# Four token groups taken by pairs, with seven block products for eight, in a fused attention and channel-MLP kernel

## The chip, the cores and the metric

One core of a Trainium2 chip runs the whole program. The metric is the device time of one execution in microseconds. Three executions of the kernel before took 926.74, 927.08 and 929.66 us; the median, 927.08 us, is the time to compare with. About 0.3% (2.8 us) is what a measurement of this kernel can tell from no change.

## The reference

Inputs are eight batches of 576 tokens. Attention has 8 heads of 64 and is cut into chunks of 64 tokens; its output `x` (576 tokens by 512 channels) goes through a low-rank token mixer and a two-layer channel network:

```python
scores = scale * (q_c @ k_c^T)               # per chunk of 64 tokens
attn = softmax(scores); out = attn @ v_c
x = out.transpose(0, 2, 1, 3).reshape(B, S, 512)
h = xt @ U @ V                               # rank 32, over the tokens; xt is x transposed
u = x + h
out = u + relu(u @ w_ch1) @ w_ch2            # 512 -> 2048 -> 512
```

U, V and the two weight matrices come as float64 words, which the kernel rounds to float32 itself.

## The kernel before, in words

**Tiles and groups.** Batches go in four pairs. A pair has 1152 tokens: 9 tiles of 128, or 3 groups of 384. The 2048 hidden channels are 16 blocks of 128, numbered f. For a group and a block, `hidden` (L850) makes 128 hidden channels by 384 tokens in one PSUM bank, `relu_high` (L858, ScalarE) and `relu_low` (L863, VectorE) evacuate it, and `project_out` (L876) adds the block's share to three open output banks. There are 12 groups, so 192 such blocks.

**Three products for one.** TensorE takes float32r. To keep float32's precision each operand is split into a high part (a rounded copy, a CAST on ScalarE) and a low part (the difference, on VectorE), and a product is three matmuls: high by high, high by low, low by high. So `hidden` is 4 slices of 128 input channels x 3 = 12 matmuls of 384 columns, and `project_out` is 3 tiles x 3 = 9 matmuls of 512 columns. All split weights stay in SBUF (`w1[f]`, `w2[f]`), with no more transfers after the first stage.

**Order of the work.** The first 32 blocks are ordered by a planner (`order`), together with the loads, the weights' rounding and the first pair's attention. After it the program is written block by block. A tick is a quarter of a block (`now` counts them, 4 to a block, 64 to a group) and `agenda` holds what else is recorded at a tick: the attention of the later pairs (`Tile`), the mixer (`Mix`, `project_ops`), and their transfers. `at(s, ...)` books a step. In each engine's queue instructions run in the order in which they were recorded.

**Attention of a later pair.** `permute` reorders q and k through DRAM, `load` reads them (L699), `turn` transposes in 32x32 blocks on VectorE (L707), `visit` makes the scores of two tiles and the values of the two before (L724, L777), `softmax`, `turn_ex`, `put_ex` and `get_ex` bring the exponentials through DRAM into the transposed form. `load_v` (L714) is issued by POOL. The fourth pair's visits stand at ticks 410, 454, 518, 538 and 582; the fourth pair's own groups run from tick 576.

**The last four groups** are group 2 of the third pair and groups 0 to 2 of the fourth: 64 of the 192 blocks, from tick 512 on. They run as all others do.

## Time and profile before

| What | Value |
|---|---|
| median of three runs | 927.08 us |
| span of the profiled execution | 927.1 us |
| TensorE busy | 908.8 us, 98% |
| VectorE busy | 455.5 us, 49% |
| ScalarE busy | 226.0 us, 24% |
| GpSimd busy | 84.7 us, 9% |
| DMA | 100.09 MB, mean 108 GB/s |

The profiled execution's span and the median differ by less than 0.1 us, so a sum made against the span can be read against the median. PE stands for TensorE, PEld for its weight loads, DVE for VectorE, ACT for ScalarE, POOL for GpSimd, and L with a number is a line of the kernel. A busy PE is not PE at its peak: matmuls overlap, so the time of one is read from the distance between two starts, not from its length.

### The profile page before, as it was taken

To read this page: it belongs to the slowest core of one execution; us is meant where nothing else is said; L and a number is where in the kernel's file an instruction comes from. 1 tells how busy PE (TensorE), PEld (TensorE's weight loads), DVE (VectorE), ACT (ScalarE), POOL (GpSimd) and SP (SyncE) were. 2 spreads that over 40 slices of the span, in tenths; PEclk is the share of its full clock that TensorE was granted. 3 is DMA by queue.
4 is the path that set the end of the run, shared out by engine and by line. 5 is a ranking of instruction groups with operands and counts; after the bars stand their busy time and mean duration, and the time that the engine had idled before them with its cause. 6 is when DMAs were issued, how large, how long until landed. Compare 5 with 4: busy or idle time off the path is not lost.

```text
span 927.1 us, 16326 instructions
## 1 busy us (share of the span) xinstructions
PE 908.8 (98%) x6596; PEld 806.3 (87%) x6596; DVE 455.5 (49%) x901; ACT 226.0 (24%) x399; POOL 84.7 (9%) x157
## 2 busy tenths in 40 slices
PE   6899999999999999999999999999999999999998
PEld 5568888888888888998898888998889889898987
DVE  4799995575455445426554455433554342321111
ACT  5576751121221221111221211111121121111110
POOL 4300000222021020202021001020103000000000
PEclk9999999999999999999999999999999999999999
DMA  9894695776387373433567546152517102110000
GB/s 181 189 322 136 155 226 103 151 197 125 53 186 164 52 175 79 108 62 102 76 148 165 89 99 169 40 131 58 103 23 168 38 3 67 57 46 1 35 1 35
DMA packets 281115, 100.09 MB, mean 108 GB/s; under 512 B 206448, under 2 KB 268432, under 8 KB 281040
## 3 DMA queue, kind: packets, MB, share of 16 engines
q1 hardware_dynamic: 165440, 76.19, 33.2%
q10 hardware_dynamic: 111360, 14.16, 9.7%
q0 software_dynamic: 4240, 8.71, 3.7%
q8 instruction: 52, 0.85, 0.4%
q14 instruction: 23, 0.19, 0.1%
HBM read 74.63 MB, written 38.54 MB: 122 GB/s over the span
## 4 chain that ended last, share of the span: by engine, by line
PE 88%; DMA 4%; DVE 3%; ACT 2%; issue 2%; SPq 1%; POOL 1%; ACTq 0%; POOLq 0%
PE o L876 41%; PE h L850 41%; DMA qkv<-in_q_dram 3%; PE as L724 2%; PE as L777 1%; DMA qkv<-in_v_dram 1%; PE u L637 1%; DVE wroom L106 1%; PE y L591 1%; PE y L590 1%; SPq L423 1%; DVE wraw L103 1%; ACT w L375 1%; DVE x L888 0%; ACT wraw L96 0%
## 5 line engine op out<-in xcount | busy, mean ns | idle before, releaser
L850 PE MATMUL h<-uth,w 128*128 128x384 f32 x1536 | 423.7, 338 | 0.0
L876 PE MATMUL o<-w,hh 128*128 128x512 f32 x1152 | 362.9, 396 | 0.6 <-ACT hh L858 0.5
L850 PEld LDWEIGHTS h<-uth,w 128*128 128x128 f32 x1536 | 281.1, 188 | 8.0 <-issue 0.2
L863 DVE SCALAR_TENSOR_TENSOR hl<-h,hh 128x384 fp32r<-128x384 f32 x192 | 106.3, 554 | 366.2 <-ACT hh L858 366.2
L850 PE MATMUL h<-utl,w 128*128 128x384 f32 x768 | 259.6, 338 | 0.0
L876 PEld LDWEIGHTS o<-w,hh 128*128 128x128 f32 x1152 | 213.3, 188 | 37.6 <-ACT hh L858 1.6
L876 PE MATMUL o<-w,hl 128*128 128x512 f32 x576 | 227.7, 395 | 0.6 <-DVE hl L863 0.5
L858 ACT ACTIVATE hh<-h 128x384 fp32r<-128x384 f32 x192 | 93.8, 489 | 547.8 <-PE h L850 542.3
L850 PEld LDWEIGHTS h<-utl,w 128*128 128x128 f32 x768 | 144.2, 188 | 8.3 <-issue 0.2
L876 PEld LDWEIGHTS o<-w,hl 128*128 128x128 f32 x576 | 108.2, 188 | 28.0 <-DVE hl L863 2.5
L714 POOL DMA_DIRECT2D vn<-in_v_dram x108 | 65.9, 619 | 603.1 <-DVE sm L750 131.7
L744 ACT ACTIVATE ex<-ex 128x512 f32<-128x512 f32 x27 | 17.1, 632 | 82.5 <-DVE ex L738 77.2
L737 DVE TENSOR_REDUCE mx<-as 128x4 f32<-128x256 f32 x54 | 22.5, 416 | 27.2 <-PE as L777 25.6
L888 DVE TENSOR_TENSOR x<-o,x 128x512 f32<-128x512 f32 x48 | 30.3, 679 | 1.7 <-PE o L876 1.7
L707 DVE STREAM_TRANSPOSE qT<-qn 128x512 f32<-128x512 f32 x27 | 19.0, 705 | 22.3 <-DMA qn<-qblocks 17.4
L643 DVE TENSOR_TENSOR x<-u,x 128x512 f32<-128x512 f32 x36 | 23.9, 669 | 6.6 <-PE u L637 6.6
L840 DVE TENSOR_TENSOR utl<-uf,uth 128x512 fp32r<-128x512 f32 x30 | 19.8, 675 | 11.4 <-ACT uth L839 11.3
L738 DVE TENSOR_TENSOR ex<-as,mx 128x256 f32<-128x256 f32 x54 | 22.9, 424 | 1.9
L839 ACT CAST uth<-uf 128x512 fp32r<-128x512 f32 x30 | 18.3, 618 | 21.2 <-DMA uf<-xs 21.1
L812 DVE STREAM_TRANSPOSE xb<-x 128x512 f32<-128x512 f32 x30 | 21.2, 708 | 0.7
L93 ACT ACTIVATE wroom<-wraw 128x1024 f32<-128x1024 f32 (+1 forms) x19 | 19.0, 998 | 8.9 <-issue 4.8
L707 DVE STREAM_TRANSPOSE kT<-kn 128x512 f32<-128x512 f32 x27 | 18.6, 690 | 4.6 <-DMA kn<-kblocks 4.2
(89 smaller groups left out, 505.8 us busy)
## 6 DMA issues: line engine op xcount, KB each, us to landing
wraw<-in_moe_w_ch_dram SPq DMA_DIRECT2D x32, 512.0 KB, 6.0
out_dram<-x SPq DMA_DIRECT2D x36, 256.0 KB, 2.3
xs<-xb SPq DMA_DIRECT2D x120, 64.0 KB, 1.8
uf<-xs SPq DMA_DIRECT2D x30, 256.0 KB, 3.3
qblocks<-in_q_dram ACTq DMA_DIRECT2D x24, 288.0 KB, 4.0
kblocks<-in_k_dram ACTq DMA_DIRECT2D x24, 288.0 KB, 5.1
vn<-in_v_dram POOLq DMA_DIRECT2D x108, 64.0 KB, 3.6
exs<-exb SPq DMA_DIRECT2D x108, 64.0 KB, 2.2
```

Source lines behind the costliest of these rows:

```text
L643: nc.vector.tensor_add(x, st["u"], x)
L707: nc.vector.transpose(dst.rearrange("p a b -> p (a b)"), src.rearrange("p a i d -> p (a i d)"))
L714: nc.gpsimd.dma_start(self.vn[e * C : (e + 1) * C, c], v[b + 2 * self.pr, HP * e : HP * (e + 1), s0 : s0 + C, :].rearrange("h s d -> s h d"),)
L737: nc.vector.reduce_max(mx[:, e], self.sc[e].rearrange("p (h k) -> p h k", k=C), axis=AX.X)
L738: nc.vector.tensor_sub(self.ex[:, e].rearrange("p b h k -> p h b k"), self.sc[e].rearrange("p (h b k) -> p h b k", b=2, k=TB), mx[:, e].un ...
L812: nc.vector.transpose(self.xb.rearrange("p g (c t) -> p c g t", t=TB), x_of[self.pr, self.t].rearrange("p (c g k) -> p c g k", g=NQ, k=TB),)
L840: nc.vector.tensor_sub(ul, self.uf, uh)
L850: nc.tensor.matmul(ps[:, :GN], lhsT=w[:, z, cc], rhs=u[:, cc, :], start=(n == 0), stop=(n == 3 * NCC - 1))
L858: nc.scalar.activation(hh, ps[:, :GN], AF.Relu)
L863: nc.vector.scalar_tensor_tensor(hl, ps[:, :GN], 0.0, hh, op0=ALU.max, op1=ALU.subtract)
L876: nc.tensor.matmul(acc[j], lhsT=h[:, js], rhs=w2[f][:, z], start=(first and i == 0), stop=(final and i == 2),)
L888: nc.vector.tensor_add(x, ps, x)
```

## The change

**Block products.** The last four groups are taken as two pairs of groups (`JOINT`, s = 0 and 1). For two blocks of hidden channels (2i and 2i+1), two halves of 256 input channels and two groups, plain work needs 8 products of 256 channels x 128 x 384. The new code forms sums and differences of the weight quarters and of the token quarters and needs 7 (k = 1 to 7), each 6 matmuls of 384 columns. The results are joined in PSUM: ScalarE copies a partial sum out of a bank (`snap`, L1453), VectorE adds it onto another bank (`add`, L1456), and the next product goes on accumulating in the bank that was copied.

**Weights' sums.** `combos` forms them on POOL (three of the 16 first adds on VectorE) in the 64 ticks before tick 512 and writes them to DRAM as float32. In the joint part each of 2 x 4 x 14 products streams one 128x256 piece back (`issue`, 11 buffers deep) and splits it (`split_w`): a CAST on ScalarE (L1366), and a subtraction (L1367), 107 of 112 times on POOL. `Combos` does the same for the tokens' sums (POOL) and their 21 splits per pair (ScalarE L1418, VectorE L1419).

**A chunk.** A joint part is 4 chunks of 4 hidden blocks. `STEPS` gives the order on PE: A and B are the two pairs of hidden blocks, the digit is the product, Ga and Gb are the output matmuls (6 each, 12 steps).

**Attention.** The fourth pair's visits move to ticks 366, 394, 420, 446 and 480, the third pair's from 218 to 390 become 221.5 to 346. Tiles of `x` of both pairs are written to DRAM (`spill`) and read again (`fetch`, `store`, `residual`), since there are only 9 buffers. `turn` and `turn_ex` transpose in place. A table (`TUNE`) shifts single steps and names the issuing queue of single transfers.

The core of the diff:

```diff
...
+        "cget 0.1.0": -16, "cget 0.1.1": -6, "cget 1.0.0": -16, "cget 1.0.1": -17,
+        "clo 0.1.2": "S", "clo 0.1.5": "S", "clo 1.0.3": "S", "clo 1.0.6": "S", "clo 1.2.3": "P",
...
+    JOINED = 8 * NF * 4
+    LOADS = 11
+    AHEAD = 5
...
+    STEPS = "A1 A5 A2 A6 A3 B1 A7 B5 A4 B2 B6 B3 Ga0 B7 Ga1 B4 Gb0 Gb1 Ga2 Gb2 Ga3 Gb3 Ga4 Gb4 Ga5 Gb5".split()
+    CHUNKS = NF // 4
+    JOINT = [((2, 2), (3, 0)), ((3, 1), (3, 2))]
...
+            a, z = slice(0, KC), slice(KC, DM)
+            nc.gpsimd.tensor_sub(r1[:, a], two[:, a], one[:, a])
+            nc.gpsimd.tensor_sub(r2[:, z], two[:, z], two[:, a])
+            nc.gpsimd.tensor_sub(r2[:, a], two[:, z], r1[:, a])
+            nc.gpsimd.tensor_sub(r1[:, z], one[:, z], r2[:, a])
+
+        def put():
+            done.add(("put", i))
+            if not i % 2:
+                wc[i // 2] = dram.tile([P, len(ORDER), KC], F32, name=f"wc_{i // 2}")
+            to = wc[i // 2]
+            one, two, r1, r2 = st["b"]
+            for src, ks in ((one, (1, 2)), (two[:, KC:], (3,)), (r1, (5, 4)), (r2, (6, 7))):
+                at = [ORDER.index("AB"[i % 2] + str(k)) for k in ks]
+                dma(
+                    "wput",
+                    to[:, at[0] : at[-1] + 1 : max(1, at[-1] - at[0])],
+                    src.rearrange("p (k x) -> p k x", x=KC),
+                    i,
+                )
+
...
+    def split_w(n):
+        if n >= BLOCKS_OF * len(JOINT):
+            return
+        assert ("issue", n) in done
+        done.add(("wsplit", n))
+        h, l = window(n)
+        nc.scalar.copy(h, l.bitcast(F32))
+        side("wlo", n).tensor_sub(l, l.bitcast(F32), h)
+
...
+            if k == 5:
+                self.sums[j] = slot(F32, f"us_{self.s}_{j}", (P, 2, NQ, 2, TB))
+            one, two = (self.sums[j][:, z] for z in range(2))
+            dst = {5: one, 6: two, 3: one, 7: two}[k]
+            if k == 5:
+                nc.gpsimd.tensor_add(dst, b[:, :, 0:2], half[4])
+            elif k == 6:
+                nc.gpsimd.tensor_sub(dst, one, half[1])
+            elif k == 3:
+                nc.gpsimd.tensor_sub(dst, half[2], two)
...
+            def snap(z, b, name):
+                t = st[z, name] = temp(f"{name}_{s}_{c}{z}")
+                nc.scalar.copy(t, bank_of(z, b))
+
+            def add(z, b, name):
+                nc.vector.tensor_add(bank_of(z, b), bank_of(z, b), st[z, name])
+
...
+                for step, run in (
+                    (p1, lambda z=z: snap(z, "x", "s1")),
+                    (p5, lambda z=z: snap(z, "c", "s5")),
+                    (p2, lambda z=z: add(z, "y", "s1")),
+                    (p6, lambda z=z: snap(z, "x", "u2")),
+                    (p6, lambda z=z: relu(z, 0, bank_of(z, "y"))),
+                    (p3, lambda z=z: add(z, "c", "u2")),
+                    (x1, lambda z=z: relu(z, 1, bank_of(z, "c"))),
+                    (p7, lambda z=z: snap(z, "x", "u3")),
+                    (p7, lambda z=z: last_join(z)),
+                    (x2, lambda z=z: relu(z, 3, st[z, "u3"])),
+                    (p4, lambda z=z: relu(z, 2, bank_of(z, "x"))),
+                ):
...
+                    z, k = step[0], int(step[1])
+                    n = loads[0]
+                    loads[0] += 1
+                    w = [v.rearrange("p (c f) -> p c f", c=2) for v in window(n)]
...
+                    for cc in range(2):
+                        for m, (wz, uz) in enumerate(((0, 0), (0, 1), (1, 0))):
+                            nc.tensor.matmul(
+                                ps,
+                                lhsT=w[wz][:, cc],
+                                rhs=u[uz][:, cc],
+                                start=(k in (1, 2, 5) and cc == 0 and m == 0),
+                                stop=(cc == 1 and m == 2),
+                                skip_group_check=True,
+                            )
...
+                    if n + LOADS < BLOCKS_OF * len(JOINT):
+                        at(f"issue {n + LOADS}", now, lambda n=n: issue(n + LOADS))
...
+    VISITS = [
+        (94, 1, 0), (114, 1, 2), (138, 1, 4), (158, 1, 6), (198, 1, 8),
+        (221.5, 2, 0), (262, 2, 2), (290, 2, 4), (318, 2, 6), (346, 2, 8),
+        (366, 3, 0), (394, 3, 2), (420, 3, 4), (446, 3, 6), (480, 3, 8),
+    ]
...
+    for pr, g in ((0, 2), (1, 0), (1, 1), (1, 2), (2, 0), (2, 1)):
+        for f in range(NF):
+            ps = hidden(pr, g, f)
+            hh = relu_high(pr, g, f, ps)
+            hs = hh, relu_low(pr, g, f, ps, hh)
+            for j in range(GT + 1):
+                tick()
+                if j < GT:
+                    flush(j)
+            pend = (pr, g, f, hs)
+    for n in range(7, LOADS):
+        issue(n)
+    for s, groups in enumerate(JOINT):
+        joint(s, groups)
...
```

**What moves on PE.** PE in the last groups, before: the end of a block's hidden matmuls and its output matmuls (`h` is the hidden bank, `uth` and `utl` the tokens' high and low parts, `o` an output bank, `hh` and `hl` the hidden parts; in square brackets what an instruction waits for).

```order
L850 MATMUL h_2_15_8938<-uth_2_8257,w_1649 128x384 x2
L850 MATMUL h_2_15_8938<-utl_2_8258,w_1649 128x384
L850 MATMUL h_2_15_8938<-uth_2_8257,w_1649 128x384
L876 MATMUL o_6_8588<-w_1607,hh_2_14_8925 128x512 [waits Activation_49]
L876 MATMUL o_6_8588<-w_1607,hh_2_14_8925 128x512
L876 MATMUL o_6_8588<-w_1607,hl_2_14_8927 128x512 [waits DVE_49]
L876 MATMUL o_7_8592<-w_1607,hh_2_14_8925 128x512 x2
L876 MATMUL o_7_8592<-w_1607,hl_2_14_8927 128x512
L876 MATMUL o_8_8596<-w_1607,hh_2_14_8925 128x512 x2
L876 MATMUL o_8_8596<-w_1607,hl_2_14_8927 128x512
```

PE in the second chunk of the first joint part: products 5 of B and 4 of A (`c_1B` and `x_1A` are PSUM banks, every `w` is a piece of the freed weight area that holds a split weight piece or a split token sum).

```order
L1524 MATMUL c_1B<-w_1021,w_1649 128x384 [waits DVE_49,Activation_49]
L1524 MATMUL c_1B<-w_1082,w_1649 128x384
L1524 MATMUL c_1B<-w_1021,w_1649 128x384 [waits Pool_49]
L1524 MATMUL c_1B<-w_1021,w_1649 128x384
L1524 MATMUL c_1B<-w_1082,w_1649 128x384
L1524 MATMUL c_1B<-w_1021,w_1649 128x384
L1524 MATMUL x_1A<-w_1500,w_614 128x384 [waits Activation_49]
L1524 MATMUL x_1A<-w_1550,w_614 128x384
L1524 MATMUL x_1A<-w_1500,w_951 128x384 [waits Pool_49]
L1524 MATMUL x_1A<-w_1500,w_614 128x384
L1524 MATMUL x_1A<-w_1550,w_614 128x384
L1524 MATMUL x_1A<-w_1500,w_951 128x384
```

The 12 matmuls of one bank became two products of 6 in two banks; product 4 goes on in the bank `x_1A`, and its first matmul waits for ScalarE.

**What moves on ScalarE.** ACT in the last group, before: one evacuation a block and nothing else.

```order
L858 ACTIVATE hh_2_3_8639<-h_2_3_8626 128x384 [waits DVE_49,PE_49]
L858 ACTIVATE hh_2_4_8665<-h_2_4_8652 128x384 [waits DVE_49,PE_49]
L858 ACTIVATE hh_2_5_8691<-h_2_5_8678 128x384 [waits DVE_49,PE_49]
L858 ACTIVATE hh_2_6_8717<-h_2_6_8704 128x384 [waits DVE_49,PE_49]
L858 ACTIVATE hh_2_7_8743<-h_2_7_8730 128x384 [waits DVE_49,PE_49]
```

ACT in the second chunk of the first joint part (COPY is `snap`, the CAST from `w` to `w` is the weights' split, ACTIVATE the relu).

```order
L1453 COPY s_0_1A<-x_1A 128x384 [waits PE_49]
L1366 CAST w_1607<-w_1607 128x256 [waits DMAHW1_49]
L1453 COPY s_0_1A<-c_1A 128x384 [waits PE_49,Activation_49]
L1453 COPY u_0_1A<-x_1A 128x384 [waits PE_49]
L1465 ACTIVATE hh_1A<-y_1A 128x384 [waits DVE_49]
L1366 CAST w_1649<-w_1649 128x256 [waits DMAHW3_49]
L1366 CAST w_614<-w_951 128x256 [waits DMAHW6_49,Pool_49]
L1366 CAST w_1021<-w_1082 128x256 [waits DMAHW7_49,Pool_49]
L1465 ACTIVATE hh_1A<-c_1A 128x384 [waits DVE_49]
L1453 COPY s_0_1B<-x_1B 128x384 [waits PE_49,Activation_49]
L1453 COPY u_0_1A<-x_1A 128x384 [waits PE_49,Activation_49]
L1366 CAST w_1128<-w_1160 128x256 [waits DMAHW4_49,Pool_49]
```

Copies of banks, weights' splits that wait for a transfer, and relus now stand in one queue.

**What moves on POOL.** POOL before: the last steps it has are issues of v loads.

```order
L714 DMA vn_7_7407<-in_v_dram 64x4x64 [waits DMASW3_49,DVE_49,Activation_49]
L714 DMA vn_7_7407<-in_v_dram 64x4x64 [waits DMASW4_49]
L714 DMA vn_7_7407<-in_v_dram 64x4x64 [waits DMASW5_49]
L714 DMA vn_7_7407<-in_v_dram 64x4x64 [waits DMASW6_49]
L714 DMA vn_8_7642<-in_v_dram 64x4x64 [waits DMAHW2_49,DMAHW1_49,DMAHW3_49,DMASW7_49,DMAHW4_49,DVE_49,PE_49]
L714 DMA vn_8_7642<-in_v_dram 64x4x64 [waits DMASW0_49]
```

POOL shortly before tick 512 (`wcl` and `wch` hold weights' sums, `us` tokens' sums, `uf` tokens read back; the next to last row splits a weight piece).

```order
L1313 TENSOR_TENSOR wcl<-w_1649 128x512 [waits DMAHW5_49]
L1315 TENSOR_TENSOR wch<-wcl 128x256 [waits DMAHW1_49,DVE_49,Pool_49]
L1316 TENSOR_TENSOR wch<-wcl 128x256 [waits DMAHW2_49]
L1317 TENSOR_TENSOR wch<-wcl,wch 128x256 [waits Pool_49]
L1318 TENSOR_TENSOR wch<-wcl,wch 128x256 [waits Pool_49]
L1392 TENSOR_TENSOR us_0_7136<-uf_0_6835 128x256 [waits DMAHW6_49,PE_49]
L1394 TENSOR_TENSOR us_0_7136<-us_0_7136,uf_6_7062 128x256 [waits DMAHW0_49,Pool_49]
L1396 TENSOR_TENSOR us_0_7136<-uf_6_7062,us_0_7136 128x256 [waits DVE_49,Pool_49]
L1398 TENSOR_TENSOR us_0_7136<-uf_6_7062,uf_0_6835 128x256 [waits DVE_49,Pool_49]
L1367 TENSOR_TENSOR w_1353<-w_1353,w_1306 128x256 [waits DMAHW2_49,Activation_49]
L1392 TENSOR_TENSOR us_1_7166<-uf_1_7052 128x256 [waits DMAHW7_49,DVE_49]
L1394 TENSOR_TENSOR us_1_7166<-us_1_7166,uf_7_7106 128x256 [waits DMAHW5_49,Pool_49]
```

Additions and subtractions between SBUF tiles, many of them waiting for the one before, now stand between and behind the issues of v loads.

## Rows read from the trace of the kernel before

**Rows 1.** The page's span, and its busy time by engine.

```profile
span 927.1 us, 16326 instructions
...
PE 908.8 (98%) x6596; PEld 806.3 (87%) x6596; DVE 455.5 (49%) x901; ACT 226.0 (24%) x399; POOL 84.7 (9%) x157
```

**Rows 2.** The page's chain that ended last, by line.

```profile
PE o L876 41%; PE h L850 41%; DMA qkv<-in_q_dram 3%; PE as L724 2%; PE as L777 1%; DMA qkv<-in_v_dram 1%; PE u L637 1%; DVE wroom L106 1%; PE y L591 1%; PE y L590 1%; SPq L423 1%; DVE wraw L103 1%; ACT w L375 1%; DVE x L888 0%; ACT wraw L96 0%
```

**Rows 3.** Windows of the span: columns as in its head.

```profile
core 0: us, PE busy (x) PEld busy (x) DVE busy (x) ACT busy (x) POOL busy (x), PEclk, DMA share, GB/s
0.00:60.00 60.00, 46.92 (x745) 33.36 (x745) 40.78 (x110) 36.02 (x62) 18.84 (x49) 1.00 0.96 222
60.00:160.00 100.00, 98.74 (x490) 87.44 (x489) 87.89 (x119) 55.28 (x75) 0.00 (x0) 1.00 0.64 168
160.00:640.00 480.00, 479.89 (x3612) 431.13 (x3611) 232.81 (x489) 89.16 (x173) 53.70 (x88) 1.00 0.53 116
640.00:760.00 120.00, 120.00 (x944) 107.35 (x943) 55.57 (x119) 23.63 (x46) 12.22 (x20) 1.00 0.34 73
760.00:927.00 167.00, 163.21 (x813) 147.01 (x811) 38.42 (x65) 21.90 (x44) 0.00 (x0) 1.00 0.12 34
```

**Rows 4.** Waits in total: us, times, longest us.

```profile
DVE qT L707 <- DMA qn<-qblocks: 17.4, 8, 4.9
...
PE ps_qT L435 <- DMA qkv<-in_q_dram: 8.3, 5, 4.2
```

**Rows 5.** Timeline of two blocks near the end: start us, us, engine, line.

```profile
906.24 0.62 PE L876 MATMUL o<-w,hh 128*128 128x512 f32 x2
906.44 0.49 ACT L858 ACTIVATE hh<-h 128x384 fp32r<-128x384 f32 x1 [3.72 <-PE h L850]
...
908.34 0.34 PE L850 MATMUL h<-uth,w 128*128 128x384 f32 x1
...
910.45 0.62 PE L876 MATMUL o<-w,hh 128*128 128x512 f32 x2
...
912.54 0.34 PE L850 MATMUL h<-uth,w 128*128 128x384 f32 x1
```

**Rows 6.** Windows, instructions of L850 alone: us, PE busy (x), PEld busy (x), PEclk, DMA, GB/s.

```profile
637.00:927.00 290.00, 145.51 (x768) 136.50 (x768) 1.00 0.21 50
```

**Rows 7.** Instruction groups of ACT: busy us, mean ns of one, idle before.

```profile
L858 ACT ACTIVATE hh<-h 128x384 fp32r<-128x384 f32 x192 | 93.8, 489 | 547.8 <-PE h L850 542.3 <-DMA qblocks<-in_q_dram 3.7 <-DVE hl L863 1.6
...
L278 ACT CAST ust<-uroom 128x320 fp32r<-128x320 f32 x4 | 1.5, 460 | 0.0
```

**Rows 8.** Instruction groups of DVE that are nearest to the new ones.

```profile
L863 DVE SCALAR_TENSOR_TENSOR hl<-h,hh 128x384 fp32r<-128x384 f32 x192 | 106.3, 554 | 366.2 <-ACT hh L858 366.2
...
L840 DVE TENSOR_TENSOR utl<-uf,uth 128x512 fp32r<-128x512 f32 x30 | 19.8, 675 | 11.4 <-ACT uth L839 11.3
...
L789 DVE TENSOR_TENSOR x<-as,sm 128x256 f32<-128x256 f32 x54 | 19.9, 414 | 0.9 <-PE as L777 0.9
```

**Rows 9.** Instruction groups of POOL: a v load's issue, and a computation.

```profile
L714 POOL DMA_DIRECT2D vn<-in_v_dram x108 | 65.9, 619 | 603.1 <-DVE sm L750 131.7 <-PE as L724 120.2 <-PE as L777 117.3
...
masks.py:199 POOL TENSOR_SCALAR_AFFINE_SELECT ident<-ident 128x128 f32<-128x128 f32 x1 | 0.3, 286 | 0.0
```

**Rows 10.** DMA issues: KB each, median us to landing.

```profile
wraw<-in_moe_w_ch_dram SPq DMA_DIRECT2D x32, 512.0 KB, 6.0
out_dram<-x SPq DMA_DIRECT2D x36, 256.0 KB, 2.3
...
uf<-xs SPq DMA_DIRECT2D x30, 256.0 KB, 3.3
...
kn<-kblocks SPq DMA_DIRECT2D x24, 256.0 KB, 4.7
```

**Rows 11.** Timeline of the tail: the last adds and the last matmul.

```profile
921.84 2.09 DVE L888 TENSOR_TENSOR x<-o,x 128x512 f32<-128x512 f32 x3 [1.70 <-PE o L876]
...
922.81 0.40 PE L876 MATMUL o<-w,hl 128*128 128x512 f32 x1
```

More of the change, by code (lines that the diff above doesn't have):

```diff
@@ L86 @@
     w2 = {}
+    area = {}
+    whole = {}
     LOW_STEP = 0.9375 * 2.0**-29 * (1.0 - 2.0**-10)
@@ L840, in split @@
             nc.vector.tensor_sub(ul, self.uf, uh)
+            done.add(("ut", self.pr, self.g, self.j))
     def hidden(pr, g, f):
+        assert all(("ut", pr, g, j) in done for j in range(GT)), (pr, g)
+        done.add(("hidden", pr, g, f))
         uh, ul = ut_of[pr, g]
@@ L869, in project_out @@
         hh, hl = hs
+        if j == GT - 1:
+            done.add(("out", pr, g, f))
         t = g * GT + j
@@ L1030, with plan_far_mix @@
-    chain.append(((NPAIR - 1) * PAIR + TIMES[0], []))
+        m, n = Mix(pr, t), f" {pr}.{t}"
+        at("mix" + n, s, m.low_rank, m.add)
+        at("mturn" + n, s + 1, m.turn)
+        at("put" + n, s + 2, m.put)
+        at("get" + n, s + 6 if get is None else get, m.get)
+        at("split" + n, s + 11 if get is None else get + 7, m.split)
+    mixes = {}
+    def plan_far_mix(pr, t, s):
+        m, n = Mix(pr, t), f" {pr}.{t}"
+        mixes[pr, t] = m
+        at("fetch" + n, s - 5, m.fetch)
+        at("mix" + n, s, m.low_rank, m.add)
+        at("mturn" + n, s + 1, m.store, m.turn)
+        at("put" + n, s + 2, m.put)
@@ new lines, with window, free, issue @@
+    ORDER = [z for z in STEPS if z[0] != "G"]
+    BLOCKS_OF = len(ORDER) * CHUNKS
+    def window(n):
+        k = n % LOADS
+        if k < 7:
+            return [area[2 * k + z][:, 3 * KC :] for z in range(2)]
+        k -= 7
+        a = area[2 * 7 + k // 2][:, (k % 2) * 2 * KC : (k % 2 + 1) * 2 * KC]
+        return [a[:, 0:KC], a[:, KC:]]
+    def free(f):
+        return ("hidden", 2, 1, f) in done and ("sum", f // 2) in done
+    def issue(n):
+        if n >= BLOCKS_OF * len(JOINT):
+            return
+        c, o = divmod(n % BLOCKS_OF, len(ORDER))
+        done.add(("issue", n))
+        assert ("put", 2 * c + (ORDER[o][0] == "B")) in done and free(min(2 * (n % LOADS), NF - 2) + 1)
+        assert n < LOADS or ("product", n - LOADS) in done
+        dma("w", window(n)[1].bitcast(F32), wc[c][:, o], n)
@@ L1032 @@
+    VISITS = [
[3 rows of a table added]
+    ]
+    chain = [(s, [Tile(pr, t) for t in range(t0, min(t0 + 2, NT))]) for s, pr, t0 in VISITS]
+    chain.append((510, []))
     made = {}
@@ L1086, with tick_of @@
+    def tick_of(n):
+        c, o = divmod(n, len(ORDER))
+        return JOINED + LENGTH // CHUNKS * c + STEPS.index(ORDER[o])
+    for n in range(BLOCKS_OF * len(JOINT)):
+        if n < 7:
+            at(f"first {n}", JOINED - 64 + 8 * n + 14, lambda n=n: issue(n))
+        at(f"wsplit {n}", JOINED - 64 + 8 * n + 19 if n < AHEAD else tick_of(n - AHEAD), lambda n=n: split_w(n))
     now = 0
```

397 lines of the change are left out of this document (306 added, 91 removed), and 152 rows, old and new, of tables (MIXES, TUNE).

## The prediction

> **What bounds the kernel now.** First the busy times: PE is busy 98% of the span, the next engine 49% [rows 1]. Then the chain of waits: output and hidden matmuls are 41% each, and all that belongs to attention, mixer and loads shares the rest [rows 2]. [...] The waits by engine confirm it: PE's longest is one for the first q loads (8.3 us in 5 waits), while VectorE waits 17.4 us for late q blocks of the later pairs without PE noticing [rows 4]. So the time is the number of matmuls times their spacing, plus the first 60 us, plus a tail. Only fewer matmuls can shorten it, and anything that makes PE wait lengthens it.
>
> The spacing comes from two neighbouring blocks: hidden matmuls start at 908.34, output matmuls at 910.45, the next hidden at 912.54 [rows 5]. That is 2.11 us for 12 matmuls of 384 columns (0.176 each), 2.09 us for 9 of 512 (0.232 each), 4.20 us for a block. The last four groups are the 768 hidden matmuls after 637 us [rows 6].
>
> **The change, part by part.**
>
> *Products removed.* 768 hidden matmuls become 2 pairs x 4 chunks x 14 products x 6 = 672. 96 x 0.176 = **-16.9 us**. Output matmuls stay 1728, attention, mixer and projection matmuls keep their counts, and those of the fourth pair only move to earlier ticks: 0, as PE pays for them wherever they stand. A chunk is then 14 x 6 x 0.176 + 12 x 6 x 0.232 = 31.5 us, eight of them 252 us.
>
> *Joins in PSUM.* New on PE are waits inside a chunk: a product accumulates in a bank that ScalarE must have copied. The tight place is product 4 after product 7, with only B5 (6 x 0.176 = 1.06 us) between. ScalarE starts 0.20 us after PE has moved on (906.24 to 906.44) and a 384-column evacuation takes 0.49 [rows 5, 7]: the bank is free after 0.69 us, 0.37 to spare. A weights' split just ahead in ScalarE's queue takes at most 0.46 (the row for 320 columns, it has 256) [rows 7], so a collision costs 0.1 us, two in a row 0.55. Other joins have two products between, 2.1 us. ScalarE's load in a chunk: 16 evacuations x 0.49 + 14 splits x 0.46 = 14.3 us, nearly all in the 17.5 us of the products: 81% full, so some collisions are sure. Lower end 0, upper 8 x 0.55 = 4.4; I take **+1**, as most chunks should find the queue free. VectorE adds 14 operations of about 0.55 [rows 8] and 6 output adds in 31.5 us, under 40%: nothing.
>
> *Weights streamed.* 112 pieces of 128 KB, each issued 11 products ahead; its CAST stands 6 products (6.3 us) behind that issue. Transfers of 256 KB land after 2.3 to 4.7 us [rows 10], so 1.6 us or more are spare: 0. The low part is subtracted on POOL, of which the trace has no two-input row. The nearest: VectorE needs 0.414 for an operation of 128x256 [rows 8], POOL 0.286 for one input of 128x128 [rows 9], so 1.15 for twice the columns and two inputs. I take 0.65 between them, since 0.41 is the same work on another engine and 1.15 other work on the same engine. Even 1.15 keeps pace: splits stand one per product, 5 products ahead, and seven of them must end before the eleven products of a stretch do, 11.6 us: up to 11.6 / 7 = 1.66 each is hidden. 0.
>
> [...]
>
> *The weights' sums and the turn to joint work.* Between ticks 448 and 512, 16 blocks or 67 us, POOL gets 13 adds of 512 columns, 32 + 12 operations of 256, about 11 splits, two subtractions of 512 and 12 v issues of 0.62 [rows 9]. At 0.65 for 256 columns and 1.25 for 512 that is 15 x 1.25 + 55 x 0.65 + 7.4 = 62 us; at the ends, 0.414 and 0.675 [rows 8] or 1.15 and 2.3, it is 40 or 105. So POOL is nearly full, each sum also waits for the one before, and the tokens' sums stand at its end. ScalarE has 9 token splits behind the last relu (9 x 0.46 = 4.1 us), which the first products need one by one while PE also does the last block's 9 output matmuls (2.1 us). Product 5 comes 1.8 us after tick 512. A few us late is likely: **+2**, from 0 to 8.
>
> *Attention moved ahead.* Both later pairs' attention must now end by tick 512, some 650 us. DMA: before, 480 x 0.53 + 120 x 0.34 = 295 us of full share from 160 to 760 us [rows 3]. Added before tick 512: 18 spills, 12 fetches, 6 stores of 0.26 MB, 7.3 MB of weights' sums, 17 MB in all; at 222 / 0.96 = 231 GB/s, the pace of the first window [rows 3], 73 us. (295 + 73) / 490 = 0.75 against 0.53. Each load has 13 ticks (14 us) for 4.7 us, and VectorE, 49% busy, gets about a quarter more: 60%. **+0.5**, from 0 to 8 (five visits late by 1.5 us). In the joint part 21 MB more are 91 of 252 us, on top of the 0.12 that the last window has: no bound.
>
> *First stage and tail.* The planner's list and its durations are the same: 0. In the tail the last matmul ends at 923.2 and the last of three adds at 923.9, 3.2 us before the end [rows 11]; add and store stay as they are: 0, give or take 0.5.
>
> *Sum.* 927.1 - 16.9 + 1 + 2 + 0.5 = **913.7 us**, -1.4%. The profiled execution is the median's equal (927.1 and 927.08), so nothing is to be scaled.
>
> **The rivals.**
>
> *1. POOL and VectorE hold each other up at the turn.* Mechanism: near tick 512 VectorE does 21 subtractions of two SBUF tiles, 0.41 each, 8.6 us in all, while POOL reads SBUF. If they cannot run side by side, POOL ends 8.6 us later, and its 5 us of room in 67 covers part: some 4 us more land on the first products, and the joint part's own 21 splits at its middle lose 2 to 3 more: 913.7 + 7 = 921. For: POOL's queue is full there. Against: nothing in this trace, where POOL only issues loads in those stages [rows 9]. [...] Chance 0.14.
>
> *2. Loads of the moved attention come late.* At 0.75 of DMA share and with sums' transfers in bursts, five visits wait 1.5 us each: 913.7 + 7.5 = 921. For: the first window, at 0.96, has all of PE's load waits [rows 3, 4]. Against: VectorE's 17.4 us of waits for q blocks cost PE nothing. Chance 0.10.
>
> *3. Slower: late weights block ScalarE's queue.* A CAST that waits for its piece holds the copies and relus behind it, and with them the product that needs the bank. It decides when a piece takes over 6.3 us from issue to landing, issue behind other SP waits included; loads of 512 KB in the crowded first stage took 6.0 us [rows 10], so it is not excluded. At 8 us about two joins in a product stretch lose 1.5 us each: 8 x 3 = 24 us, 913.7 + 24 = 938. Against: 4.7 us is the slowest of the 256 KB medians [rows 10]. Chance 0.08.
>
> *4. POOL's splits are too slow.* Beyond 1.66 us each, a stretch lengthens by 7 x (t - 1.66); at 2.3 it is 4.5 us a chunk, 36 us: 950, slower as well; at 2.0 it just eats the gain. Against: the upper bound of 1.15. Chance 0.06.
>
> **How the numbers follow.** The forecast has 0.62, the rivals 0.14, 0.10, 0.08 and 0.06. A measurement tells 0.3% (2.8 us) from no change. Forecast and rivals 1 and 2 are all faster by more than that: 0.86. Of rivals 3 and 4, 0.03 lies about where the loss eats the gain, 0.11 beyond. The range begins where no new wait costs anything, 927.1 - 16.9 = 910.2, less 0.7 for a shorter tail: 909.5. Upward it takes in rivals 1 and 2 up to 921.5, which leaves rivals 3 and 4 out.
>
> **What would show it.** Right: 672 matmuls of the products, spaced 0.176; a PE window of 31 to 32 us per chunk; PE's idle time of the last stage within 4 us, most of it in the first chunk, ended by ScalarE or POOL. The joint sum is wrong if PE's waits for ScalarE come in every chunk; the turn is wrong if the first chunk alone loses over 8 us or nothing; rival 2 shows as PE waiting at visits between 450 and 650 us, rival 3 as ScalarE CASTs ended by DMA, rival 4 as products ended by POOL with a subtraction over 1.6 us. The saving itself is wrong if product matmuls are spaced wider than hidden ones were.

## The result, and the profile after

The changed kernel takes 932.2 us (median of 14 runs, 929.95 to 935.31), the kernel before 927.33 in the same rounds (14 runs, 925.48 to 932.02): ratio 1.0052, interval 1.0040 to 1.0065. It is slower by 0.5%, where 913.7 with a range of 909.5 to 921.5 was forecast. The profiled execution has a span of 930.5 us. Every time listed with its core's span lies 1.8 us above it, so a trace need not be of a typical execution: the changed kernel's is at its median, the one before (span 927.1, so about 928.9) some 1.6 us above its median, those of the half visits and of the closed y bank below are of the fastest executions, those of the two best versions of the slowest. By that distance the agreement of 927.1 and 927.08 ahead of the prediction was chance; of the 4.9 us between the medians the two spans show 3.4.

The page of the changed kernel, span, busy times and the chain by engine, to be held against [rows 1]:

```profile
span 930.5 us, 17207 instructions
...
PE 896.5 (96%) x6500; PEld 788.0 (85%) x6500; DVE 525.8 (57%) x1011; ACT 292.3 (31%) x602; POOL 250.0 (27%) x361
...
PE 75%; DVE 10%; DMA 5%; issue 3%; POOL 2%; ACT 2%; SPq 2%; ACTq 0%; DVEq 0%; POOLq 0%
```

TensorE has its 96 matmuls less (6500 for 6596) and 12.3 us less busy time (896.5 for 908.8), but its idle time went from 18.3 to 34.0 us, and VectorE is now 10% of the chain. The windows of the changed kernel, same columns as [rows 3], say where:

```profile
0.00:60.00 60.00, 48.32 (x748) 35.04 (x749) 41.53 (x111) 36.11 (x63) 19.21 (x49) 1.00 1.01 237
60.00:160.00 100.00, 99.01 (x493) 88.17 (x493) 86.70 (x119) 54.76 (x74) 4.89 (x8) 1.00 0.63 164
160.00:640.00 480.00, 467.51 (x3845) 414.15 (x3844) 259.00 (x550) 92.33 (x178) 107.57 (x150) 1.00 0.66 154
640.00:680.00 40.00, 36.51 (x209) 31.81 (x209) 23.69 (x41) 16.29 (x44) 32.43 (x40) 1.00 0.64 186
680.00:760.00 80.00, 80.00 (x398) 71.78 (x397) 39.43 (x67) 30.82 (x80) 28.08 (x39) 1.00 0.54 163
760.00:927.00 167.00, 165.17 (x815) 147.09 (x814) 75.43 (x127) 61.99 (x164) 57.78 (x76) 1.00 0.23 74
```

From 160 to 640 us TensorE was idle 0.1 us before [rows 3]; now 12.5. The turn to the joint part costs 3.5 (640 to 680 us), and the joint part itself is full. TensorE's waits by what ended them, in us in total, times, longest:

```profile
PE h L1097 <- DVE x L985: 7.4, 8, 1.7
PE ps_qT L609 <- DMA qkv<-in_q_dram: 5.5, 3, 4.2
PE o L1125 <- ACT hh L1105: 2.2, 2, 1.7
PE ps_eT L609 <- ACT ex L662: 1.9, 3, 0.9
PE y L1016 <- DVE xl L1002: 1.6, 2, 1.2
PE y_0A L1524 <- ACT s_0A L1453: 1.6, 1, 1.6
...
PE as L973 <- DMA eT<-exs: 1.3, 2, 0.8
PE o L1125 <- DVE hl L1110: 1.3, 2, 0.9
PE x_3B L1524 <- ACT u_3B L1453: 1.1, 1, 1.1
```

The largest row is new: a hidden block waits eight times for the scaling operation of an attention visit (L985). The longest of them, on TensorE and then on VectorE (start us, us, engine, line, in brackets the idle time before and who ended it):

```profile
395.28 1.14 PE L973 MATMUL as<-vn,eT 64*64 64x64 f32 x64
398.12 0.42 PE L1097 MATMUL h<-uth,w 128*128 128x384 f32 x1 [1.69 <-DVE x L985]
398.37 0.34 PE L1097 MATMUL h<-utl,w 128*128 128x384 f32 x1
```

```profile
395.96 0.42 DVE L931 TENSOR_REDUCE mx<-as 128x4 f32<-128x256 f32 x1 [2.21 <-PE as L973]
396.42 0.42 DVE L932 TENSOR_TENSOR ex<-as,mx 128x256 f32<-128x256 f32 x1
396.77 0.41 DVE L931 TENSOR_REDUCE mx<-as 128x4 f32<-128x256 f32 x1
397.21 0.42 DVE L932 TENSOR_TENSOR ex<-as,mx 128x256 f32<-128x256 f32 x1
397.56 0.75 DVE L985 TENSOR_TENSOR x<-as,sm 128x256 f32<-128x256 f32 x2
```

The visit's four banks hold scores and values; the first of them is read last by the first of two scalings (397.56 to 397.97), and the hidden block starts right behind. In the kernel before such a block does not wait. There, on TensorE and on VectorE:

```profile
646.40 1.18 PE L777 MATMUL as<-vn,eT 64*64 64x64 f32 x64
647.51 0.73 PE L876 MATMUL o<-w,hh 128*128 128x512 f32 x2
648.08 0.39 PE L876 MATMUL o<-w,hl 128*128 128x512 f32 x1
648.31 0.34 PE L850 MATMUL h<-uth,w 128*128 128x384 f32 x1
```

```profile
648.67 0.74 DVE L789 TENSOR_TENSOR x<-as,sm 128x256 f32<-128x256 f32 x2
```

The hidden block starts at 648.31, before the scaling does (648.67), so it writes another bank. A bank is one of the eight PSUM tiles of 128x512 float32 that the program hands out for TensorE's results (`bank`, from a pool of eight). The bank numbers that the two programs assign, around one visit of each beside the same group's hidden blocks, say the same (a star: one of the visit's four):

```
before  visit [2, 7, 3, 0]  hidden block ahead 5   hidden block behind 5
after   visit [3, 6, 7, 1]  hidden block ahead 1*  hidden block behind 3*
```

Three output banks, four of the visit and one for y are all eight. The y bank collects the projections of five tiles of `x` for the mixer. Before, these five stood in a row, after the pair's fifth tile and again after its ninth (`plan_proj`), so y was closed during visits. In the changed kernel `Tile.project` stands six ticks after each visit, so y stays open from a pair's first tile on. Behind 12 of its 16 visits, and behind none before, the next hidden block gets a bank of the visit.

A ledger of TensorE's time from the start of its first matmul to that of its last, worked out from its timeline: each matmul's count times its pitch (0.175 us for 384 columns, 0.230 for 512, 0.110 and 0.122 for 128 and 144, 0.0161 for attention's 64), the waits, and the rest, which is matmuls that start late without a wait or run slower, as the first ones behind a wait do (behind the 1.69 us at 398 us the first two hidden matmuls start 0.25 apart for 0.175, behind the 1.69 us at 664 us the first three output matmuls take 1.06 for 0.69, both at a granted clock of 1.00):

| us | pitch x count | waits | rest |
|---|---|---|---|
| before | 880.6 | 9.5 | 28.5 |
| after | 863.8 | 24.9 | 33.0 |
| of it 160 to 640 us, before / after | 473.1 / 455.8 | 0 / 12.2 | 6.9 / 12.1 |
| of it 640 to 680 us | 39.1 / 34.9 | 0 / 3.5 | 0.9 / 1.6 |
| of it after 680 us | 240.2 / 243.6 | 0 / 1.1 | 2.7 / 1.2 |

The saving is there (-16.8, 96 matmuls at 0.175). Waits took 15.4 of it back and the rest 4.5: +3.1, and with a tail that is 0.3 longer the span grew by 3.4.

### The profile page after: what moved, and what is told of

It is laid out like the page before. It is cut to its first block, busy times and chain, and to the rows that moved or that the text cites. A ratio compares the mean times of both kernels' runs of the same rounds, so it can differ in the third digit from the quotient of the medians.

```text
span 930.5 us, 17207 instructions
## 1 busy us (share of the span) xinstructions
PE 896.5 (96%) x6500; PEld 788.0 (85%) x6500; DVE 525.8 (57%) x1011; ACT 292.3 (31%) x602; POOL 250.0 (27%) x361
## 4 chain that ended last, share of the span: by engine, by line
PE 75%; DVE 10%; DMA 5%; issue 3%; POOL 2%; ACT 2%; SPq 2%; ACTq 0%; DVEq 0%; POOLq 0%
PE h L1097 23%; PE o L1125 22%; PE o L1499 14%; DMA qkv<-in_q_dram 2%; PE as L918 1%; DVE ex L932 1%; DVE mx L931 1%; PE x_0B L1524 1%; PE x_2B L1524 1%; PE x_1B L1524 1%; PE x_1A L1524 1%; PE x_2A L1524 1%; DVE wraw L271 1%; DVE wroom L274 1%; DVE w L1419 1%
## 5 line engine op out<-in xcount | busy, mean ns | idle before, releaser
L1097 PE MATMUL h<-uth,w 128*128 128x384 f32 x1024 | 282.6, 339 | 7.4 <-DVE x L985 7.4
L1125 PE MATMUL o<-w,hh 128*128 128x512 f32 x768 | 242.8, 397 | 2.2 <-ACT hh L1105 2.2
L1097 PEld LDWEIGHTS h<-uth,w 128*128 128x128 f32 x1024 | 187.4, 188 | 15.8 <-issue 11.0
L1097 PE MATMUL h<-utl,w 128*128 128x384 f32 x512 | 173.1, 338 | 0.5 <-DVE utl L1084 0.5
L1125 PEld LDWEIGHTS o<-w,hh 128*128 128x128 f32 x768 | 141.5, 188 | 27.4 <-ACT hh L1105 3.5
L1125 PE MATMUL o<-w,hl 128*128 128x512 f32 x384 | 152.1, 396 | 1.3 <-DVE hl L1110 1.3
L1097 PEld LDWEIGHTS h<-utl,w 128*128 128x128 f32 x512 | 96.2, 188 | 5.7 <-DVE utl L1084 0.8
L1125 PEld LDWEIGHTS o<-w,hl 128*128 128x128 f32 x384 | 72.2, 188 | 20.3 <-DVE hl L1110 3.4
L1367 POOL TENSOR_TENSOR w<-w,w 128x256 fp32r<-128x256 f32 x70 | 52.7, 767 | 71.1 <-ACT w L1366 68.4
L1367 POOL TENSOR_TENSOR w<-w 128x256 fp32r<-128x256 f32 x37 | 27.6, 753 | 70.0 <-ACT w L1366 69.9
L1366 ACT CAST w<-w 128x256 fp32r<-128x256 f32 x112 | 41.8, 409 | 13.7 <-DMA w<-wc 9.0
L898 DVE STREAM_TRANSPOSE qn<-qn 128x512 f32<-128x512 f32 x27 | 19.0, 703 | 12.7 <-DMA qn<-qblocks 12.5
```

The lines of the kernel that those rows point to most:

```text
L1097: nc.tensor.matmul(ps[:, :GN], lhsT=w[:, z, cc], rhs=u[:, cc, :], start=(n == 0), stop=(n == 3 * NCC - 1))
L1125: nc.tensor.matmul(acc[j], lhsT=h[:, js], rhs=w2[f][:, z], start=(first and i == 0), stop=(final and i == 2),)
L1366: nc.scalar.copy(h, l.bitcast(F32))
L1367: side("wlo", n).tensor_sub(l, l.bitcast(F32), h)
```

## The experiments

The theories: **A**, the open y bank takes the spare PSUM bank from the hidden block behind a visit; **B**, VectorE has too much to do in the middle; **C**, transfers crowd each other. Later **D**, single instructions stand in the wrong order in in-order queues, and **E**, the engines' work as such is the bound. All ratios are against the kernel before. A run whose interval overlaps the changed kernel's 1.0040 to 1.0065 is not told apart from it by its time: that holds for the earlier visits, the half visits, the closed y bank and the splits at the turn. The edits are shown shortened.

**Early projection alone.** The kernel before, with one line changed:

```
-  plan_proj(pr, e, i, s + i)
+  plan_proj(pr, e, i, made[pr, i + 4 * e] + 2 + (i + 4 * e) % 2)
```

> The kernel before, with one thing of the change alone: the projection of each tile is issued two to three ticks after its attention visit instead of five tiles in a row after the fifth tile, so the accumulating y bank stays open through the visits of a pair (3 output banks, 1 y bank and 4 banks of the visit are all 8). Attention is not moved ahead, the eight plain products stay, no weights' sums. Theory A (the open y bank takes the spare PSUM bank, so the hidden block behind a visit gets one of the visit's own banks and waits until VectorE's scaling has emptied it): TensorE waits 'h <- DVE x' appear in some 8 to 10 visits, 4 to 8 us together (none in the kernel before), and the time rises by 3 to 8 us, to 930 to 935. Theory B (VectorE has more to do in the middle because the attention was moved ahead): the middle holds no more work than before, so no such wait, time within 1 us of 927. Theory C (transfers crowd each other when attention is moved ahead): as B, within 1 us.

Measured: 940.0 us, 1.0133 (1.0110 to 1.0157), more than A's upper end. TensorE's waits in it:

```profile
PE h L850 <- DVE x L789: 9.0, 11, 1.3
PE ps_qT L435 <- DMA qkv<-in_q_dram: 6.0, 3, 4.2
PE sc L466 <- ACT qkT L458: 1.5, 2, 0.9
```

The row that is new in the changed kernel comes up here with nothing else of the change in it: no weights' sums, no attention moved ahead, no products removed. The banks that this version assigns agree: behind 11 of its 16 visits the next hidden block stands on one of the visit's, and there are 11 such waits. B and C fall as its first cause.

**The same, VectorE's visit bank by bank.** On top of it, in `visit` (with `softmax` and `scaled` cut by bank):

```
-    now[z].softmax()
-    prev[z].scaled()
+    for e in range(2):
+        now[z].softmax(e)
+        prev[z].scaled(e)
```

> The kernel before with early projection (e1_early_y) and VectorE's work in a visit bank by bank. Same work as the kernel before. Theory A (the open y bank leaves no spare bank, the hidden block waits for the visit's first bank): the 9.0 us of 'h <- DVE x' fall to 0 to 2 us, and the time from 940 to 929 to 933. Theory F (the early projections themselves, their splits and their place between other products, make the 13 us): the time stays within 3 us of 940.

Measured: 932.9 us, 1.0059 (1.0043 to 1.0075), within A's 929 to 933. The row `h <- DVE x` fell from 9.0 to 1.0 us and 7 of the 13 us came back, by order alone. So the wait is for the bank. The other 5 to 6 us of early projection have another cause: in this execution (span 930.6) TensorE's waits are only 1.3 us above those before, and another 2.3 are matmuls that start late or run slower; what makes the rest is not settled.

**The changed kernel, VectorE's visit bank by bank.** The same edit.

> The changed kernel, with VectorE's work in a visit in another order only: bank by bank (maximum, subtraction, scaling of bank 0, then of bank 1) instead of both softmax halves and then both scalings, so the visit's first bank comes free after three VectorE operations instead of five. Same work, same banks, same transfers, y bank still open. Theory A: the hidden block behind a visit, which stands on the visit's first bank, finds it free about two operations (some 0.8 to 1 us) earlier; the 7.4 us of 'h <- DVE x' waits fall to 0 to 2 us, and the time by 4 to 8 us, to 924 to 928. Theory B (VectorE's load as such) and theory C (transfers): VectorE has the same sum to do and the transfers are the same, so the waits move to other tiles and the time stays within 1.5 us of 932.

Measured: 928.92 us, 1.0021 (1.0005 to 1.0037): 3.3 us less than the changed kernel, under A's 4 to 8. The waits show a part of why:

```profile
PE ps_qT L609 <- DMA qkv<-in_q_dram: 6.8, 4, 4.1
PE y L1019 <- DVE xl L1005: 4.4, 4, 2.4
PE o L1128 <- ACT hh L1108: 2.3, 2, 1.9
...
PE h L1100 <- DVE x L988: 1.4, 2, 0.9
```

The bank wait fell by 6.0 us, as A has it, but the wait of the projection for its low part (`y <- DVE xl`) rose from 1.6 to 4.4: TensorE now comes to the projection before VectorE has worked off what stands behind the visit. Behind the longest of these waits the granted clock was 0.76, 0.50 and 0.88 in the three windows of 2 us from 436 us, by estimate from these 3.4 us at half (last section).

**Visits one or two places earlier,** away from the next hidden block:

```
+  early = s - max(0, int(s) % 4 - 1)
-  agenda.setdefault(int(s // 1), []).append((s, ...))
+  agenda.setdefault(int(early // 1), []).append((early, ...))
```

> The changed kernel, with every visit that stands one output product or none ahead of the next hidden block (10 of 16) put one or two places earlier, so that two output products (some 1.4 us of TensorE) stand between a visit and the next hidden block. Banks, work and transfers are unchanged, the y bank stays open. In the changed kernel's trace a visit with no product behind it waits 1.69 us, with one 0.7 to 0.8, with two 0 to 0.5. Theory A: the 7.4 us of 'h <- DVE x' waits fall to 1 to 3 us and the time by 3 to 6 us, to 926 to 929. Theory B or C: VectorE's backlog and the transfers are as before, so the wait is only met elsewhere: within 1.5 us of 932.

Measured: 931.1 us, 1.0035 (1.0018 to 1.0051), hardly a gain; A's 926 to 929 is missed, and by its time alone B or C would hold. `h <- DVE x` fell from 7.4 to 1.0, as A says, and `o <- DVE hl` rose from 1.3 to 3.3: the low half of the rectifier now stands in VectorE's queue behind the visit's operations (eight of them ahead of the longest wait, 1.97 us). The first stage's load waits were 2 us longer in this execution as well.

**Half visits.** Two visits of one tile, four ticks apart, with two banks each:

```
-  at s: visit(prev, now)
+  for z in range(2):
+      at s + 4 * z: visit(prev[z : z + 1], now[z : z + 1])
```

> The changed kernel, with each visit of two tiles cut into two visits of one tile, the second one hidden block (four ticks) later, with its loads, turns, splits and projection. A visit then opens two banks instead of four, and with the y bank open two banks are left over. Same work and same number of transfers. Theory A: no 'h <- DVE x' wait is left (7.4 us in the changed kernel), and the time falls by 6 to 10 us, to 922 to 926, below the kernel before. Theory B: VectorE's load in the middle is the same, so waits of the same sum come up at the halves: within 2 us of 932. Theory C: the second tile's transfers have more time, the first's the same: a fall of at most 2 us.

Measured: 930.55 us, 1.0030 (1.0014 to 1.0047); the profiled execution has a span of 925.5. No `h <- DVE x` wait is left, as A says, but its time of 922 to 926 is missed; B's, within 2 us of 932, holds. New is a wait of 2.5 us: VectorE stands at a transpose that waits 5.21 us for a load put off by this edit, and `hl` behind it:

```profile
180.75 0.71 DVE L898 STREAM_TRANSPOSE qn<-qn 128x512 f32<-128x512 f32 x1 [5.21 <-DMA qn<-qblocks]
181.55 0.71 DVE L898 STREAM_TRANSPOSE kn<-kn 128x512 f32<-128x512 f32 x1
182.19 0.98 DVE L1110 SCALAR_TENSOR_TENSOR hl<-h,hh 128x384 fp32r<-128x384 f32 x2
```

**The y bank closed for pairs 1 and 2.** The changed kernel, y emptied by VectorE after every one or two tiles:

```
+  if shut and last:
+      if (pr, e) not in y_of: nc.vector.tensor_copy(y_of[pr, e], ps)
+      else: nc.vector.tensor_add(ps if i == 4 else y_of[pr, e], ps, y_of[pr, e])
```

> The changed kernel, with the y bank of pairs 1 and 2 emptied after every one or two tiles: VectorE adds the partial sum up in the tile that later holds the split sum, so no y bank stays open through a visit, and a fifth bank is free behind every visit of these pairs; pair 3 keeps its open bank. The partial sums are rounded to the tile's type, which changes the numbers slightly; VectorE gets 12 operations of 128x512 more (about 0.65 us each). Ticks, transfers and the order of VectorE's visit work are unchanged. Theory A (the open y bank takes the spare bank): of the eight 'h <- DVE x' waits the six of pairs 1 and 2 (0.80, 0.69, 0.52, 1.69, 0.80, 0.80) go, the two of pair 3 (1.27, 0.80) stay: 2 us instead of 7.4; time down by 3.5 to 6 us, to 926 to 929. Theory B (VectorE's load): VectorE has 8 us more to do, so the waits grow: 932 to 936.

Measured: 934.47 us, 1.0077 (1.0063 to 1.0090), 2.3 us above the changed kernel, with intervals that overlap. On the waits A holds: with a fifth bank the waits beside an open y bank of pairs 1 and 2 are gone (seven and not six, since the one of 1.27 us, counted to pair 3, stood beside pair 2's bank), and one of 0.8 us is left in pair 3. On the time A is wrong, and B's 932 to 936 holds though its waits did not grow. TensorE's waits at the top of the list:

```profile
PE y L1020 <- DVE xl L1002: 4.8, 4, 2.2
PE as L973 <- DMA eT<-exs: 2.3, 3, 0.9
PE y_0A L1537 <- ACT s_0A L1466: 1.6, 1, 1.6
```

`y <- DVE xl` is at 4.8 us again, and the granted clock of the runs is 0.994 to 0.997, against 0.995 to 1.000 in the changed kernel. Two waits stand one behind the other at an early projection: for the bank, and, once that is cured, for VectorE's queue behind the visit; that twelve more operations make this queue longer is argued. A names what the eight waits are for; it does not by itself name what they cost. The trace does not show where the 2.3 us went: its span is 928.9, 1.6 less than the changed kernel's, and its waits are 2.4 us less.

**The splits at the turn.** The changed kernel, six shifts of the table:

```
-  "csplit 0.1.5": -0.75, "csplit 0.1.7": 5.75, "csplit 0.2.3": 1.25, "csplit 0.2.7": 1.25
+  "csplit 0.1.5": 1.25, "csplit 0.1.7": 9.5, "csplit 0.2.3": 5.25, "csplit 0.2.7": 6.25, "csplit 1.0.3": 1, "csplit 1.2.3": 1
```

> The changed kernel, with six splits of the joint groups' block sums (one of k=5, one of k=3 and two of k=7 at the start of the joint part, two of k=3 a quarter before its middle) issued later, behind the copies and rectifiers that stood behind them in ScalarE's queue. Same work. Theory D (ScalarE's queue is in order: casts that wait for GpSimd's sums hold the rectifier and the copies that TensorE waits for): the waits of 1.69 (o <- ACT hh), 1.57 (y_0A <- ACT s_0A) and 1.11 us (x_3B <- ACT u_3B) go, and the time falls by 2.5 to 4.5 us, to 927.5 to 930. Theory E (GpSimd's and VectorE's sum of work at the turn is the bound): the late sums are then missed by the products that need them, other waits of the same sum come up, and the time stays within 1 us of 932.

Measured: 931.08 us, 1.0037 (1.0024 to 1.0050). The three waits are gone but for 0.2 (of 4.6 us after 640 us, 1.4 are left), but the time fell by 1.1 only, and other waits grew (`as <- DMA eT` from 1.3 to 2.1, the first stage's for q and k from 6.1 to 7.6). That lies between D's 2.5 to 4.5 and E's under 1; the order of ScalarE's queue makes these waits, its price in time is not settled. In this execution the granted clock also fell to half for 3.4 us at two waits for exponentials (0.90 and 1.17 us), by estimate 1.7 us, which does not happen in the changed kernel's trace. The mechanism as it stands in the changed kernel, on ScalarE, the first row a cast that GpSimd's sum held up, the second the rectifier for which TensorE waited 1.69 us:

```profile
663.26 0.40 ACT L1418 CAST w<-us 128x256 fp32r<-128x256 f32 x1 [1.07 <-POOL us L1392]
663.57 0.48 ACT L1105 ACTIVATE hh<-h 128x384 fp32r<-128x384 f32 x1
```

**Two versions that beat both kernels.** The half visits, with the second tile's loads not put off, its exponentials out and back ahead of the weights' sums' stores in SyncE's queue, and the turn's splits later:

```
-  at("load " + a.n, o + (start if z == 0 else s - 13), a.load)
+  at("load " + a.n, (start if z == 0 else s - 13), a.load)
-  at("eget " + a.n, o + max(s1 + 7, after - 12) + z, a.get_ex)
+  at("eget " + a.n, max(o + s1 + 7, after - 12) + z, a.get_ex)
```

> The half visits (e3_half_visits) with three more edits of order: the second tile's loads are not put off with its half visit, its exponentials go out and come back ahead of the stores of the weights' sums in SyncE's queue, and the same splits at the turn are issued later. Same work. Left in the half visits' trace: o <- DVE hl 2.5 us at 183 us, where VectorE's transpose stood waiting 5.2 us for a load, followed by 3 to 4 us at the low clock level; as <- DMA eT 2.2 us; y_0A <- ACT s_0A 1.6; x_3B <- ACT u_3B 1.1. Theory D (what is left are orders in the in-order queues of VectorE, SyncE and ScalarE): these four go, and the time falls by 6 to 9 us against 930.6, to 921 to 925, below the kernel before. Theory E (VectorE, GpSimd or the transfers are the bound as such): the waits come up elsewhere; within 2 us of 930.

Measured: 924.22 us, 0.9968 (0.9955 to 0.9980). And the bank-by-bank order with later projections and splits:

```
+  "project 1_2": 2, "project 1_3": 2, "project 2_2": 2, "project 2_4": 2, "project 2_5": 2, "project 3_2": 2.0
```

> The bank-by-bank order (e4_bank_order) with six projections issued two ticks later (those for whose low part TensorE waited 0.4 to 2.4 us, the last followed by a stretch at granted clock 0.85) and the same splits at the turn issued later. Same work. Theory D (what was left there are orders in in-order queues): y <- DVE xl falls from 4.4 to under 1 us, the waits at the turn from 4.6 to under 1.5, and the time by 5 to 8 us against 928.9, to 921 to 924. Theory E (VectorE's sum of work is the bound in the middle): VectorE's low parts are only met later; within 1.5 us of 929.

Measured: 924.18 us, 0.9962 (0.9949 to 0.9976). Both are faster than the kernel before by 0.3 to 0.4% and than the changed kernel by 8 us, from edits of order alone. On the time D's forecast holds for the first (921 to 925) and is just missed by the second (921 to 924). On the waits it holds in part: in the first `as <- DMA eT` is still at 1.9 and a wait of 3.54 us for ScalarE's rectifier is new, in the second `y <- DVE xl` is at 1.8, not under 1, and the turn at 1.8, not under 1.5. The traces do not show what the 6 us of the first are: its span is 924.8 for the half visits' 925.5, its waits 17.2 us for 15.9.

**More of the same.** Three more shifts for the half visits (`csplit 0.1.5`, `project 3_2`, `eget 1_8`), and fourteen for the other (`visit 2_4`, two `project`, four steps each of tiles 3_6 and 3_7, three `csplit`):

> The second half-visit kernel (e7_halves2) with three more shifts: the split of k=5 that stood ahead of the last rectifier in ScalarE's queue (o <- ACT hh 3.54 us at 660 us, with granted clock 0.96 behind it) goes behind it, one projection two ticks later (y <- DVE xl 1.52 us), one read of exponentials two ticks earlier (as <- DMA eT 1.39 us). Same work. Theory D (orders in in-order queues): 5 to 7 us of waits and low clock go, 924.2 becomes 918 to 920. Theory E (the engines' work as such): waits of the same sum come up elsewhere, within 1.5 us of 924.

> The second bank-by-bank kernel (e8_order2) with more shifts: one visit with no output product behind it a tick or two earlier (h <- DVE x 0.9 us), two projections two ticks later (y <- DVE xl 1.4 us), the last exponentials' way out and back three to four ticks earlier (as <- DMA eT 1.6 us), three splits at the turn later (x_0A <- ACT u_0A 0.9 us). Same work. Theory D: some 4 us of waits go, 924.2 becomes 920 to 922. Theory E: within 1.5 us of 924.

Measured: 924.52 us, 0.9970 (0.9958 to 0.9982), and 925.72 us, 0.9979 (0.9966 to 0.9992). By the time E holds, in the second but for 0.2 us. In the first's trace TensorE's waits are fewer (13.7 us for 17.2) though the median stayed. In the second a wait moved away by hand comes up elsewhere: the exponentials that were to come earlier came later (`as <- DMA eT` 3.7 us, one of 3.1), and a rectifier's low half waited 1.25 us.

## Why the prediction was wrong

**Products removed** was right: 672 matmuls where 768 were, spaced 0.175, and a joint chunk is full but for its joins. The clause at its end was not: that attention and projection matmuls moved to earlier ticks cost nothing, since TensorE "pays for them wherever they stand". Their place decides which PSUM banks are open beside them. The sum started from the span, so 913.7 is a span too and about 915.5 a time; the miss stays.

**Joins in PSUM** (+1, from 0 to 4.4) measured 1.1, at one join in eight chunks. Right, and at the place that was named, product 4 behind product 7; the casts ahead of the copy there were those of the tokens' sums, though, not the weights'.

**Weights streamed** (0) was right: no wait of TensorE was ended by a weights' load. GpSimd's two-input operation, bounded by 0.41 and 1.15 and taken as 0.65, measured:

```profile
L1367 POOL TENSOR_TENSOR w<-w,w 128x256 fp32r<-128x256 f32 x70 | 52.7, 767 | 71.1 <-ACT w L1366 68.4
```

That is 0.77 in the mean, far from 1.66.

**The weights' sums and the turn** (+2, from 0 to 8) measured 3.5 us of waits. The size was about right and the mechanism half: GpSimd's sums were late and ScalarE's casts waited for them, but what TensorE lacked was a rectifier (1.69 us) and a copy (1.57) behind those casts, not the splits that the first products need (0.24). Nor was GpSimd full: the sum ahead of the late copy had itself waited 1.90 us for VectorE's split. Between ticks 448 and 512 (590.5 to 668 us) GpSimd was busy 55 of 77 us.

**Attention moved ahead** (+0.5, from 0 to 8) is the step that failed. It was costed by shares: DMA 0.75 and VectorE 60%. Both came out lower, 0.66 and 54% (259 of 480 us) from 160 to 640 us, and the stage still lost 12.2 us of waits, and 5.2 us of matmuls that start late or run slower beside them. Of the waits 7.4 us are for a PSUM bank, which no share of an engine shows, 3.5 for results of VectorE that stood late in its queue and 1.3 for late exponentials. That early projection does this on its own is shown by the kernel before with that line alone (+12.8 us); that the wait is for the bank by two edits that take it away, another order on VectorE (9.0 to 1.0) and a fifth bank (seven of eight waits gone). Curing the bank alone returned 3.3 us by the order and nothing by the fifth bank; that VectorE's queue is the next wait is shown, that it makes up the whole difference is not.

**First stage and tail** (0) came out as -1.3 us of waits in the first stage, by one execution each, and 0 behind 680 us apart from the join; these waits lie between 5.9 and 9.5 us in the traces of all the other versions, so no effect is shown. In its rivals the prediction looked for late loads: `as <- DMA eT` is 1.3 us in two waits (rival 2 priced five of 1.5). Rival 3's first half occurred: two of ScalarE's casts stood waiting for their weights' piece, 4.75 and 4.25 us; no wait of TensorE followed. (The slowest median of 256 KB in the trace before was 5.6 us, of the first k loads, not 4.7.) Slow splits (rival 4) did not occur; by that rival's own terms splits of 2.0 us would have cost 19 us, more than the gain. Rival 1 has its mechanism in the trace, within the term for the turn. VectorE's split of 128x256 there, the shortest, median and longest in ns:

```profile
L1419 DVE TENSOR_TENSOR w<-us,w x23: 408/626/979, 658.0 to 796.6; 128x256 fp32r<-128x256 f32 x23
```

It took 0.41 us where GpSimd computed nothing (668.3 us) and 0.98 where GpSimd computed all the while (670.1). What that cost TensorE is not shown. None of the four is what made the kernel slower, and the chance of 0.11 for slower came from the wrong two.

**What stays open.** The best versions are at 924.2, not 913.7. In the ledger of the second bank-by-bank version the saving is whole (-16.8), but waits are 16.9 for 9.5 and the rest 35.0 for 28.5, of which a stretch of 3.4 us at half clock is, by estimate, 1.7. Whether an order exists in which these go, or whether VectorE's and GpSimd's work around the visits sets a floor, the last two runs leave undecided. A version with the projections in rows of five again, as before, was not tried: pairs 2 and 3 store their tiles away.

## What to carry to other kernels

When a step moves, list what it holds open until its end (accumulators, buffers) and count those against what runs beside it in the new place; busy shares of engines and DMA do not show it (here VectorE at 54% and DMA at 0.66 in the stage that lost 12.2 us to waits). Where all banks are taken, the next user waits for the operation that empties the oldest (here a hidden block behind a visit, eight times, 7.4 us), so order that engine's work bank by bank, and then look for the next wait in its queue before expecting the time back. Tell a saving in matmuls and a cost in waits apart by a ledger of the bound engine; it shows at once whether the saving failed or was spent.
